# Small vectors on the ScalarE queue, the first key tile masked out of PSUM, and a table of priority offsets for the list scheduler

## Chip, cores and metric

The kernel runs on one core of a Trainium2 chip. The time is device microseconds of one execution; the median of three runs before the change is 300.35 us (300.14 to 301.22).

## What is computed

A token gate g mixes two branches over x (2048 tokens, 512 features). Branch A is attention with 32 heads of 16 in four segments of 512 tokens, plus a memory carried from segment to segment; branch B is a gated MLP with 1792 hidden features.

```python
g = sigmoid((x * gate_w).sum(-1, keepdims=True))
# branch A, per segment s; phi(t) = t + 1 if t > 0 else exp(t); gb = sigmoid(beta), one per head
p = softmax(qs @ ks.T * 0.25 + causal_mask);  a_dot = p @ vs
a_mem = (phi(qs) @ M) / (phi(qs) @ z + 1e-6)
o_s = gb * a_mem + (1 - gb) * a_dot
M += phi(ks).T @ vs;  z += phi(ks).sum()
a = concat(o_s) @ wo
# branch B
b = (gelu(x @ w_gate) * (x @ w_up)) @ w_down
return g * a + (1 - g) * b
```

## The kernel before

Everything works on one segment of 512 tokens at a time, features or heads on the 128 partitions. All work is written as tasks with reads and writes; a list scheduler, `Sched.schedule` (run while the kernel is built), picks for the earliest free engine the ready task with the highest priority, which is the longest chain of estimated times behind it plus the task's `bias`. The order that comes out is then fixed: each engine runs its own list in order and waits on semaphores where a task needs another engine. So whatever stands behind a waiting instruction on its engine waits too.

The tasks, by the functions in which they are written:

- `prep(s)`: projections K, Q (transposed, feature by token) and V, by `proj_T` and `pieces`, matmuls of line 408 into one of three rotating PSUM buffers `psW`, evicted by `copy_out` on ScalarE (line 422) or VectorE (line 425). K is then masked twice by `kp` (line 589 in the first segment, 597 later) into `kpad_0` and `kpad_1`, so that one 32-row matmul serves one head of two. The token gate (`gate`, `gexs`, `gts`), the transposed factors `exsT` (GpSimd) and `GdT`, and from the second segment on phi of Q (`pqe`, `pqc`), the denominator `den` (matmuls 128x8, then `ndsc` on VectorE) and four numerators `num` (matmuls 128x128, each evicted as `otok` on VectorE, line 657, and transposed by DMA into `oT`).
- `memory(s)`: phi of K, its DMA transposes `phkt`, the memory matmuls `mz` (128x136), added up and masked on VectorE (`mzacc`, `mzbd`).
- `attention(s)`: for each of four feature tiles t five passes A0, B0, C, A1, B1. A pass is score matmuls (`qk`, line 710) into the four banks `psXALL`, one exp of 128x2048 on ScalarE (line 718), and a causal mask on GpSimd (line 730). After B0 and C, and at the end, `pv` (line 743) multiplies with V into `psP`, VectorE transposes it (`tb`, line 751), and after both halves `norm` normalises: `recip`, `sc`, `obf`, `ott` and the add into `oT`, five VectorE instructions, lines 763 to 771.
- `gates_copied`, `gelu_phase`, `ups`, `downs`: the MLP, gate `G` (weights wg), gelu in one block per stage on ScalarE, up `U` (wu) with the product `Um` on VectorE (line 841), and down `D` together with the output projection (wd, wo), evicted as `ost` with the gate as scale (lines 866, 869).

The four stages are the four attentions; MLP and projections of the neighbouring segments fill TensorE between the passes.

At the start all loads stand in SP's list in the order of `rank`: x in two pieces, wk, wq, wv, then the small vectors `gatew`, `betab` (beta on every partition) and four `betaT` (beta in the order of the transposed heads), then the MLP weights (lines 438, 439) and the transposing loads of the second segment's x. `gexp` and `gexpT` (lines 546, 547) are exps of beta on ScalarE, counted among the first stage's exps so that one table load serves all; `gmat` is a chain of five VectorE operations behind them (lines 550 to 555).

Of the kernel before, what the change touches and what calls it, by code (L numbers as in the profile page):

```python
# [2 lines left out]

# [3 lines left out]
PE, ACT, DVE, POOL, SP = "pe", "act", "dve", "pool", "sp"  # L7
# [4 lines left out]
ACTF = mybir.ActivationFunctionType  # L12
# [7 lines left out]
P = 128  # L20
# [5 lines left out]
DMA_RATE = 330.0e3  # L26
PATIENCE = 3.0
OPEN_BONUS = 6.0
HOP = {PE: 0.17, ACT: 0.07, DVE: 0.07, POOL: 0.10, SP: 0.0}


# [38 lines left out]
class Task:  # L70


    def __init__(self, name, alts, grp=None, after=(), bias=0.0, nbytes=0):
        self.name = name
        self.alts = alts
        self.grp = grp
        self.after = tuple(after)
        self.bias = bias
        self.nbytes = nbytes
        self.tiled = None  # L80
        self.patience = 0.0
        self.ahead = False
        self.est = {e: sum(i.est for i in l) for e, l in alts.items()}
        rs, ws = set(), set()
        for l in alts.values():
            for i in l:
                rs.update(i.reads)
                ws.update(i.writes)
        self.reads, self.writes = rs, ws
        self.preds, self.succs = set(), set()  # L90
        self.prio = 0.0
        self.eng = None
        self.start = self.finish = None
        self.id = None
# [223 lines left out]
def act_t(n, psum=True, ap=False):  # L318
    return (0.167 if psum else 0.20) + n / 1200.0 + (0.093 if ap else 0.0)
# [15 lines left out]
def _build(es, nc, A_x, A_wq, A_wk, A_wv, A_wo, A_beta, B_w_gate, B_w_up, B_w_down, gate_w, out):  # L335
# [68 lines left out]
    def task(name, eng, instrs, **kw):  # L404
        return S.add(Task(name, {eng: instrs}, **kw))
# [12 lines left out]
    def copy_out(name, g, dst, src, reads, writes, n, engs=(ACT, DVE), **kw):  # L418

        alts = {}  # L420
        if ACT in engs:
            alts[ACT] = [Instr(lambda e: e.activation(dst(), src(), ACTF.Copy), reads=reads, writes=writes,
                               est=act_t(n))]
        if DVE in engs:
            alts[DVE] = [Instr(lambda e: e.tensor_copy(dst(), src()), reads=reads, writes=writes,  # L425
                               est=dve_t(n))]
        return S.add(Task(name, alts, grp=g, **kw))

    def dma(name, eng, out_ap, in_ap, reads, writes, nbytes, issue=0.7, transpose=False, bias=0.0, sm=None,
            nonc=False):  # L430
        sm = sm if sm is not None else sem("d")

        def f(e):
            if transpose:
                return e.dma_start_transpose(out_ap(), in_ap())
            if nonc:
                with nc.allow_non_contiguous_dma(reason="small vector"):
                    return e.dma_start(out_ap(), in_ap())  # L438
            return e.dma_start(out_ap(), in_ap())  # L439
        return task(name, eng, [Instr(f, reads, writes, issue, dma_sem=sm)], bias=bias, nbytes=nbytes)  # L440
# [3 lines left out]
    def wdma(key, eng, dst, src, nbytes, nonc=False):  # L444
        rank[0] -= 20.0
        dma("w_" + str(key), eng, lambda: dst, lambda: src, [], [("w", key)], nbytes, bias=rank[0], nonc=nonc)
# [28 lines left out]
    wdma("wk", SP, wk[:], r4(A_wk), 524288)  # L475
    wdma("wq", SP, wq[:], r4(A_wq), 524288)
    wdma("wv", SP, wv[:], r4(A_wv), 524288)
    wdma("gatew", SP, gatew[:], gate_w.rearrange("(kb p) -> p kb", p=P), 1024, nonc=True)
    wdma("beta", SP, betab[:], A_beta.partition_broadcast(P), 8192)
    for g in range(4):  # L480
        bsrc = A_beta.rearrange("(t g j) -> g t j", g=4, j=2)[g]
        rank[0] -= 20.0
        dma(f"betaT{g}", SP, lambda g=g: betaT[32 * g:32 * g + 32, :].rearrange("p (t j) -> p t j", j=2),
            lambda bsrc=bsrc: bsrc.partition_broadcast(32), [], [("betaT", g)], 1024, nonc=True, bias=rank[0])
    wdma(("wg", 0), SP, wg[:, :, 0:half], wgr[:, :, 0:half], 917504)
    wdma(("wg", 1), SP, wg[:, :, half:DF], wgr[:, :, half:DF], 917504)
    xdma(1)
# [67 lines left out]
        Instr(lambda e: e.tensor_tensor(gmat[:], gexp[:], gtmp[:], ALU.mult), [("c", "gexp"), ("c", "gtmp")],  # L555
              [("c", "gmat")], 0.2)])

    def proj_T(name, s, t, w, wkey, dst, wkeys):

        g = Grp(banks)  # L560
        xs = xT[s % NX]
        pieces(name, g, [mm(g, lambda: g.f32()[:, :], w[:, kb, t * 128:(t + 1) * 128], xs[:, kb, :],
                            [("xT", s % NX, kb), ("w", wkey)], kb == 0, kb == 3, 512) for kb in range(4)], 2)
        copy_out(name + "ev", g, lambda: dst[:, t, :], lambda: g.f32()[:, :], [g.key], wkeys, 512)

    def phi_task(nm, s, phase, src, skey, dst, dkey, i):
# [15 lines left out]
    def prep(s):  # L582
        sl, x3 = s % 2, s % NX
        ph = max(s - 1, 0)
        for t in range(4):
            proj_T(f"K{s}_{t}", s, t, wk, "wk", kT, [("kT", t)])
            if s == 0:
                task(f"kp{s}_{t}", DVE, [
                    Instr(lambda e, t=t, j=j: e.tensor_scalar(kpad[j][sl][:, t, :], kT[:, t, :], maskc[j][:, 0:1],
                                                              None, ALU.mult),  # L590
                          [("kT", t), ("c", "mask", j)], [("kpad", j, sl, t)], dve_t(512, 4, ap=True))
                    for j in range(2)])
            proj_T(f"Q{s}_{t}", s, t, wq, "wq", qT[sl], [("qT", sl, t)])
        if s > 0:
            for j in range(2):
# [385 lines left out]
```

## Time and profile before

| | |
|---|---|
| median of three runs | 300.35 us (300.14 to 301.22) |
| profiled execution, its own time | 301.33 us |
| its span, first to last instruction | 299.6 us |
| mean granted TensorE clock | 0.977 |
| busy: TensorE, ScalarE, VectorE, GpSimd | 277.6, 216.9, 192.0, 103.7 us |

A row of the trace names the line of the kernel, the engine and the tiles (output, arrow, inputs). A time in square brackets is how long the engine stood idle before, and what ended that. TensorE's clock is given as a share of 2.4 GHz; 0.50 is 1.2 GHz.

### The profile page before, as it was taken

The page shows a single profiled execution, that of the slowest core. Times are in us where ns is not written, and L with a number is a line of the kernel's source. Part 1 is how long each engine was busy: PE and PEld are TensorE (multiplying, and loading weights), DVE is VectorE, ACT ScalarE, POOL GpSimd, SP SyncE. Part 2 cuts the span into 40 slices and gives each one's busy share as a digit, 9 for nine tenths or more (in the row PEclk, how much of TensorE's full clock was granted, in tenths as well). Part 3 has the DMA queues.
Part 4 walks back from the last instruction along what each step waited for, and adds up shares of the span by engine and source line. Part 5 has one row for each costly group of instructions (what it writes and reads, how often), then busy time and mean ns, then how long its engine had stood idle before and what let it go on. Part 6 is the DMA issues. An engine that isn't in the chain of part 4 may idle for free.

```text
span 299.6 us, 5379 instructions
## 1 busy us (share of the span) xinstructions
PE 277.6 (93%) x2189; PEld 114.6 (38%) x2189; DVE 192.0 (64%) x333; ACT 216.9 (72%) x171; POOL 103.7 (35%) x193
## 2 busy tenths in 40 slices
PE   7459999999979999997899999999899999999995
PEld 3113433333434333443344433434344333343342
DVE  1036889868898864699643956479844636478440
ACT  3156988868999878796768897887878666686502
POOL 7002675434101333663200333385400334334300
PEclk9958999999999999999799999999999999999999
DMA  6299970000013421000300200100001200000002
GB/s 223 58 267 320 307 127 0 2 0 3 0 23 49 93 49 53 20 1 2 70 2 0 53 20 0 55 19 2 0 2 31 43 1 35 20 20 0 2 0 70
DMA packets 29737, 15.30 MB, mean 51 GB/s; under 512 B 21264, under 2 KB 29712, under 8 KB 29712
## 3 DMA queue, kind: packets, MB, share of 16 engines
q1 hardware_dynamic: 29712, 14.96, 20.2%
q8 instruction: 17, 0.28, 0.4%
q14 instruction: 8, 0.07, 0.1%
HBM read 8.14 MB, written 2.10 MB: 34 GB/s over the span
## 4 chain that ended last, share of the span: by engine, by line
PE 77%; DVE 7%; ACT 5%; DMA 3%; POOL 3%; SPq 2%; issue 2%; ACTq 0%; POOLq 0%
PE psW L408 62%; PE psXALL L710 8%; PE psP L743 6%; ACT pt L718 4%; DMA betaT<-in_A_beta_dram 3%; POOL pt L730 1%; SPq L439 1%; PE psXALL L408 1%; DVE otok L657 1%; POOL exsT L625 1%; DVE kpad_1 L597 1%; SPq L438 1%; DVE ndsc L646 1%; DVE hT L841 1%; DVE tb L751 0%
## 5 line engine op out<-in xcount | busy, mean ns | idle before, releaser
L718 ACT ACTIVATE pt<-psXALL 128x2048 bf16<-128x2048 f32 x80 | 150.1, 1877 | 46.2 <-PE psXALL L710 34.5
L730 POOL TENSOR_SCALAR_AFFINE_SELECT pt<-pt 128x512 bf16<-128x512 bf16 (+1 forms) x112 | 83.8, 750 | 176.1 <-ACT pt L718 167.8
L408 PE MATMUL psW<-xT,wu 128*128 128x512 bf16 x224 | 52.8, 380 | 1.0 <-DVE mzacc L683 0.7
L408 PE MATMUL psW<-xT,wg 128*128 128x512 bf16 x224 | 51.6, 381 | 0.0
L408 PE MATMUL psW<-wd,hT 128*128 128x512 bf16 x210 | 51.6, 380 | 0.0
L841 DVE TENSOR_TENSOR hT<-psW,hT 128x512 bf16<-128x512 f32 x56 | 37.5, 686 | 14.3 <-PE psW L408 14.0
L751 DVE STREAM_TRANSPOSE tb<-psP 128x512 f32<-128x512 f32 x32 | 22.8, 713 | 34.9 <-PE psP L743 34.8
L408 PEld LDWEIGHTS psW<-xT,wg 128*128 128x128 bf16 x224 | 20.6, 98 | 26.1 <-issue 2.0
L408 PEld LDWEIGHTS psW<-xT,wu 128*128 128x128 bf16 x224 | 20.1, 98 | 25.8 <-issue 2.7
L408 PEld LDWEIGHTS psW<-wd,hT 128*128 128x128 bf16 x210 | 18.6, 98 | 23.4 <-issue 4.3
L743 PE MATMUL psP<-pt,vaug 128*17 128x256 bf16 (+3 forms) x512 | 23.8, 306 | 0.6 <-POOL pt L730 0.6
L710 PE MATMUL psXALL<-qT,kpad_0 32*128 32x512 bf16 (+3 forms) x256 | 16.3, 308 | 8.1 <-DVE gtmp L553 7.3
L820 ACT ACTIVATE hT<-psW 128x512 bf16<-128x512 f32 x28 | 16.3, 597 | 6.8 <-PE psW L408 6.8
L710 PE MATMUL psXALL<-qT,kpad_1 32*128 32x512 bf16 (+3 forms) x256 | 16.1, 305 | 2.5 <-ACT pt L718 2.5
L408 PE MATMUL psW<-wv,xT 128*128 128x512 bf16 x64 | 17.8, 421 | 0.4 <-DVE vaug L425 0.4
L408 PE MATMUL psW<-xT,wq 128*128 128x512 bf16 x64 | 16.0, 381 | 0.5 <-DMA wq<-in_A_wq_dram 0.5
L425 DVE CAST hT<-psW 128x512 bf16<-128x512 f32 x22 | 14.5, 677 | 2.6 <-PE psW L408 2.5
L408 PE MATMUL psW<-wo,oT 128*128 128x512 bf16 x60 | 15.9, 380 | 0.0
L408 PE MATMUL psW<-xT,wk 128*128 128x512 bf16 x64 | 15.5, 380 | 0.2 <-DMA wk<-in_A_wk_dram 0.2
L743 PEld LDWEIGHTS psP<-pt,vaug 128*17 128x17 bf16 x512 | 10.1, 90 | 14.1 <-issue 6.8
L625 POOL COPY exsT<-exs 32x4 f32<-32x4 f32 x64 | 14.2, 222 | 3.7
L710 PEld LDWEIGHTS psXALL<-qT,kpad_0 32*128 32x128 bf16 x256 | 4.5, 92 | 25.3 <-ACT pt L718 13.2
(92 smaller groups left out, 249.9 us busy)
## 6 DMA issues: line engine op xcount, KB each, us to landing
out_dram<-ost SPq DMA_DIRECT2D x16, 128.0 KB, 1.7
wg<-in_B_w_gate_dram SPq DMA_DIRECT2D x2, 896.0 KB, 13.4
wu<-in_B_w_up_dram SPq DMA_DIRECT2D x2, 896.0 KB, 6.4
wd<-in_B_w_down_dram SPq DMA_DIRECT2D x1, 1792.0 KB, 12.7
hT<-in_A_x_dram SPq DMA_DIRECT2D x2, 256.0 KB, 2.8
wk<-in_A_wk_dram SPq DMA_DIRECT2D x1, 512.0 KB, 5.2
wq<-in_A_wq_dram SPq DMA_DIRECT2D x1, 512.0 KB, 6.2
wv<-in_A_wv_dram SPq DMA_DIRECT2D x1, 512.0 KB, 7.1
```

The source lines that it names most:

```text
L408: return Instr(lambda e: e.matmul(view(), lhsT, rhs, start=first, stop=last), reads=reads, writes=[fkey if fkey is not None else g.key], e ...
L425: alts[DVE] = [Instr(lambda e: e.tensor_copy(dst(), src()), reads=reads, writes=writes, est=dve_t(n))]
L438: return e.dma_start(out_ap(), in_ap())
L439: return e.dma_start(out_ap(), in_ap())
L625: cross = task(f"exsT{s}", POOL, [Instr(lambda e, g=g, c=c: e.tensor_copy(exsT[sl][32 * g:32 * g + 32, c:16:4], exs[32 * c:32 * c + 32, s4 ...
L710: instrs.append(Instr(lambda e, t=t, g=g, j=j, kb=kb, ncol=ncol, c0=c0: e.matmul(X[g][:, c0:c0 + ncol], kpad[j][sl][32 * g:32 * g + 32, t, ...
L718: prev_exp[0] = exp_task(s, f"exp{s}_{t}{name}", [Instr(lambda e: e.activation(PT[slot][:], XALL[:, :].rearrange("p (g c) -> p g c", g=4), ...
L730: minstrs.append(Instr(lambda e, view=view, pat=pat: e.affine_select(out=view, in_=view, compare_op=ALU.is_ge, fill=0.0, base=0, pattern=p ...
L743: instrs.append(Instr(lambda e, q=q, kb=kb, slot=slot, c0=c0, h=h: e.matmul(Pb[32 * q:32 * q + 17, 128 * kb:512], Vaug[sl][:, kb, h, :], P ...
L751: task(f"pvt{s}_{t}_{j}", DVE, [Instr(lambda e: e.transpose(Tb[i2][:, j, :], Pb[:, :]), [("P",)], [("Tb", i2, j)], dve_t(512))])
L820: lambda e, g=g, ft=ft, s=s: e.activation(hT[s % 2][:, ft, :], g.f32()[:, :], ACTF.Gelu_apprx_tanh),
L841: task(f"Um{s}_{ft}", DVE, [Instr(lambda e, g=g, ft=ft: e.tensor_tensor(hT[sl][:, ft, :], g.f32()[:, :], hT[sl][:, ft, :], ALU.mult), [g.k ...
```

## The change

Three things change.

First, the six small loads are issued by ScalarE's queue in place of SP's, and in another order: `betab`, four `betaT`, then `gatew`. ScalarE issues them before its first table load.

Second, the first K tile of the first segment is evicted twice by ScalarE: once through `kpad_0`'s mask as a scale column, straight from PSUM into `kpad_0`, and once as before into `kT`. The VectorE task that made both masks makes only `kpad_1` for that tile.

Third, a table `BIAS` of 89 numbers, keyed by the name of a task up to the first underscore or dot (kind and segment), is added to the priorities. The instructions and their sizes stay as they were.

```diff
+BIAS = {
+    "D1": 28, "D2": -81, "D3": -30, "G1": -23, "G2": -26, "G3": 129, "GdT0": 14, "GdT1": 24, "GdT3": -43,
...
-        self.bias = bias
+        self.bias = bias + BIAS.get(name[:re.search(r"[_.]|$", name).start()], 0.0)
...
-    wdma("gatew", SP, gatew[:], gate_w.rearrange("(kb p) -> p kb", p=P), 1024, nonc=True)
-    wdma("beta", SP, betab[:], A_beta.partition_broadcast(P), 8192)
+    wdma("beta", ACT, betab[:], A_beta.partition_broadcast(P), 8192)
     for g in range(4):
...
-        dma(f"betaT{g}", SP, lambda g=g: betaT[32 * g:32 * g + 32, :].rearrange("p (t j) -> p t j", j=2),
-            lambda bsrc=bsrc: bsrc.partition_broadcast(32), [], [("betaT", g)], 1024, nonc=True, bias=rank[0])
+        dma(f"betaT{g}", ACT, lambda g=g: betaT[32 * g:32 * g + 32, :].rearrange("p (t j) -> p t j", j=2),
+            lambda bsrc=bsrc: bsrc.partition_broadcast(32), [], [("betaT", g)], 1024, nonc=True, bias=rank[0],
+            issue=0.5)
+    wdma("gatew", ACT, gatew[:], gate_w.rearrange("(kb p) -> p kb", p=P), 1024, nonc=True)
...
-    def proj_T(name, s, t, w, wkey, dst, wkeys):
+    def proj_T(name, s, t, w, wkey, dst, wkeys, even=None):
...
+        if even is not None:
+            task(name + "even", ACT, [Instr(lambda e: e.activation(even[0], g.f32()[:, :], ACTF.Copy,
+                                                                   scale=maskc[0][:, 0:1]),
+                                            [g.key, ("c", "mask", 0)], [even[1]], act_t(512, ap=True))], grp=g)
...
-            proj_T(f"K{s}_{t}", s, t, wk, "wk", kT, [("kT", t)])
+            first = s == 0 and t == 0
+            proj_T(f"K{s}_{t}", s, t, wk, "wk", kT, [("kT", t)],
+                   even=(kpad[0][sl][:, t, :], ("kpad", 0, sl, t)) if first else None)
...
-                    for j in range(2)])
+                    for j in ((1,) if first else (0, 1))])
```

Where the order moves, in three places. First, ScalarE at the start of the program, before:

```order
L467 ACT_TABLE_LOAD
L467 ACTIVATE stmp<-pt 128x1
L422 ACTIVATE xT<-psW 128x512 x2
L422 ACTIVATE kT<-psW 128x512
L546 ACTIVATE gexp<-betab 128x32
L547 ACTIVATE gexpT<-betaT 128x8
L422 ACTIVATE qT<-psW 128x512
L422 ACTIVATE kT<-psW 128x512
L718 ACTIVATE pt<-psXALL 128x2048
```

and with the change:

```order
L452 DMA betab<-in_A_beta_dram 128x32
L451 DMA betaT<-in_A_beta_dram 32x4x2 x4
L451 DMA gatew<-in_gate_w_dram 128x4x1
L480 ACT_TABLE_LOAD
L480 ACTIVATE stmp<-pt 128x1
L435 ACTIVATE xT<-psW 128x512 x2
L560 ACTIVATE gexp<-betab 128x32
L561 ACTIVATE gexpT<-betaT 128x8
L579 ACTIVATE kpad_0<-psW,maskc 128x512
L435 ACTIVATE kT<-psW 128x512 x2
L738 ACTIVATE pt<-psXALL 128x2048
```

Six DMA issues stand ahead of the table load, and the exps of beta stand ahead of every eviction of K. On VectorE the five `gmat` operations now stand ahead of the cast of the first Q tile, which VectorE has in place of ScalarE; on TensorE the first score matmuls come after 12 projection matmuls and 2 of V, before after 16 projection matmuls.

Second, TensorE between the last `pv` of the first stage and the second stage's passes (psW<-xT,wu is an up projection, psW<-vaug,phkt is `mz`, psW<-mzbd,phq 128x8 is `den` and 128x128 is `num`, wd and wo are the down part), before:

```order
L408 MATMUL psW<-vaug,phkt 128x136 x16
L408 MATMUL psW<-xT,wu 128x512 x12
L408 MATMUL psW<-mzbd,phq 128x8 x16
L408 MATMUL psW<-xT,wu 128x512 x4
L408 MATMUL psW<-mzbd,phq 128x128 x16
L408 MATMUL psW<-xT,wu 128x512 x28
L710 MATMUL psXALL<-qT,kpad_1 128x384 x4
```

and with the change:

```order
L421 MATMUL psW<-xT,wu 128x512 x52
L421 MATMUL psW<-vaug,phkt 128x136 x16
L421 MATMUL psW<-gatew,xT 128x1 x16
L421 MATMUL psW<-wo,oT 128x512 x4
L421 MATMUL psW<-wd,hT 128x512 x2
L421 MATMUL psW<-wo,oT 128x512 x2
L730 MATMUL psXALL<-qT,kpad_1 128x384 x4
L730 MATMUL psXALL<-qT,kpad_1 128x128 x4
L421 MATMUL psW<-wo,oT 128x512 x2
L421 MATMUL psW<-wd,hT 128x512 x2
L421 MATMUL psW<-mzbd,phq 128x8 x16
L421 MATMUL psW<-wd,hT 128x512 x4
```

All up projections come first (the four missing matmuls stand just above), `mz` after them, and `den` and the four `num` go between down projections, after the next passes of scores. K and V of the second segment, which stood just ahead of these rows, were moved forward into the first stage.

Third, TensorE at the end of the second stage, from `den` on, before:

```order
L408 MATMUL psW<-mzbd,phq 128x8 x16
L408 MATMUL psW<-xT,wu 128x512 x6
L710 MATMUL psXALL<-qT,kpad_1 128x256 x8
L408 MATMUL psW<-mzbd,phq 128x128 x4
L408 MATMUL psW<-xT,wu 128x512 x2
L710 MATMUL psXALL<-qT,kpad_1 128x512 x4
L408 MATMUL psW<-mzbd,phq 128x128 x12
L710 MATMUL psXALL<-qT,kpad_1 128x384 x4
```

and with the change, from the last `pv` row after `den` on:

```order
L763 MATMUL psP<-pt,vaug 17x128 x4
L421 MATMUL psW<-mzbd,phq 128x128 x12
L730 MATMUL psXALL<-qT,kpad_1 128x256 x8
L421 MATMUL psW<-mzbd,phq 128x128 x4
L730 MATMUL psXALL<-qT,kpad_1 128x512 x4
L421 MATMUL psW<-xT,wu 128x512 x6
L730 MATMUL psXALL<-qT,kpad_1 128x384 x4
```

Three `num` groups come at once and take all three buffers; the next up projection stands behind the fourth. VectorE's list has one `otok`, the five instructions of `norm`, then three `otok`, in both. In the third stage K, V and Q of the last segment and 9 of the 14 up groups of the third come ahead of its end, 12 up matmuls standing between its last C and A1 scores where 6 stood; `mz`, `den` and `num` of the last segment go into the fourth stage; and at that stage's end 10 matmuls of the down part stand between the last C and A1 scores where 4 up matmuls stood.

## Rows read from the trace of the kernel before

**Rows 1.** Page, busy time of the whole span: us, share, instructions of each engine.

```profile
PE 277.6 (93%) x2189; PEld 114.6 (38%) x2189; DVE 192.0 (64%) x333; ACT 216.9 (72%) x171; POOL 103.7 (35%) x193
```

**Rows 2.** Table by stretch: busy us per engine (instructions), PEclk, DMA share, GB/s.

```profile
11.40:14.00 2.60, 0.00 (x0) 0.00 (x0) 0.00 (x0) 0.14 (x1) 0.00 (x0) 1.00 0.04 0
14.00:18.65 4.65, 0.00 (x0) 0.03 (x1) 0.53 (x4) 0.83 (x3) 0.00 (x0) 0.52 0.69 260
18.65:24.40 5.75, 5.75 (x23) 1.72 (x24) 3.79 (x10) 3.25 (x4) 0.65 (x1) 0.50 1.36 209
80.00:90.00 10.00, 7.50 (x58) 3.46 (x56) 9.74 (x20) 10.00 (x5) 0.00 (x0) 1.00 0.10 20
140.00:144.00 4.00, 0.83 (x9) 0.33 (x8) 3.93 (x6) 3.19 (x2) 1.20 (x2) 0.98 0.00 0
144.00:147.30 3.30, 3.29 (x34) 1.40 (x35) 2.75 (x5) 1.34 (x1) 0.54 (x1) 0.50 0.41 83
200.00:214.00 14.00, 12.38 (x133) 5.42 (x135) 12.54 (x22) 10.74 (x8) 8.08 (x14) 1.00 0.01 1
...
274.00:280.00 6.00, 4.85 (x32) 1.83 (x31) 5.46 (x10) 4.43 (x3) 2.86 (x3) 1.00 0.00 0
```

**Rows 3.** Chain of waits, start of the program: start, us, what.

```profile
7.22 10.48 DMA betaT<-in_A_beta_dram
```

**Rows 4.** Timeline, 0 to 24 us: start, us, engine, line, instruction, idle before.

```profile
0.81 1.28 ACT L467 ACT_TABLE_LOAD   x1 [0.81 <-PEq L966]
...
3.42 0.68 SPq L438 DMA_DIRECT2D gatew<-in_gate_w_dram  x1
...
4.14 1.60 SPq L439 DMA_DIRECT2D betab<-in_A_beta_dram  x1
...
5.78 1.87 SPq L438 DMA_DIRECT2D betaT<-in_A_beta_dram  x4
...
8.59 1.04 PE L408 MATMUL psW<-xT,wq 128*128 128x512 bf16 x4 [0.48 <-DMA wq<-in_A_wq_dram]
...
11.31 0.23 ACT L546 ACTIVATE gexp<-betab 128x32 f32<-128x32 bf16 x1 [2.56 <-DMA betab<-in_A_beta_dram]
17.82 0.21 ACT L547 ACTIVATE gexpT<-betaT 128x8 f32<-128x8 bf16 x1 [6.28 <-DMA betaT<-in_A_beta_dram]
...
18.06 0.17 DVE L550 TENSOR_SCALAR gexpT<-gexpT 128x8 f32<-128x8 f32 x1 [8.66 <-ACT gexpT L547]
...
18.65 0.62 PE L710 MATMUL psXALL<-qT,kpad_0 32*128 32x512 bf16 x4 [7.30 <-DVE gtmp L553]
18.93 0.19 DVE L555 TENSOR_TENSOR gmat<-gexp,gtmp 128x32 f32<-128x32 f32 x1
...
19.57 0.68 DVE L425 CAST qT<-psW 128x512 bf16<-128x512 f32 x1
...
22.45 1.14 SPq L439 DMA_DIRECT2D wu<-in_B_w_up_dram  x2
```

**Rows 5.** Page, DMA issues: tiles, queue, count, KB each, median us to landing.

```profile
out_dram<-ost SPq DMA_DIRECT2D x16, 128.0 KB, 1.7
...
wu<-in_B_w_up_dram SPq DMA_DIRECT2D x2, 896.0 KB, 6.4
...
hT<-in_A_x_dram SPq DMA_DIRECT2D x2, 256.0 KB, 2.8
```

**Rows 6.** Timeline of TensorE, after the first stage.

```profile
88.47 6.22 PE L408 MATMUL psW<-xT,wu 128*128 128x512 bf16 x28 [0.19 <-DVE otok L657]
```

**Rows 7.** Timeline of VectorE, end of the second stage.

```profile
137.15 0.72 DVE L751 STREAM_TRANSPOSE tb<-psP 128x512 f32<-128x512 f32 x1 [0.31 <-PE psP L743]
...
139.28 0.34 DVE L763 RECIPROCAL recip<-tb 128x32 f32<-128x32 f32 x1
...
141.47 1.29 DVE L771 TENSOR_TENSOR oT<-oT,ott 128x512 bf16<-128x512 bf16 x1
...
142.68 0.68 DVE L657 TENSOR_TENSOR otok<-psW,ndsc 128x512 bf16<-128x512 f32 x1
```

More of the change, by code (lines that the diff above doesn't have):

```diff
@@ L1 @@
+import re
 from contextlib import ExitStack
@@ L28 @@
 OPEN_BONUS = 6.0
+BIAS = {
[10 rows of a table added]
+}
 HOP = {PE: 0.17, ACT: 0.07, DVE: 0.07, POOL: 0.10, SP: 0.0}
```

9 rows, old and new, of the table BIAS are left out of this document.

## The prediction

> **What bounds the kernel now.** Read first, on the page, the shares of busy time: TensorE is busy 93% of the span [rows 1]. So two things are worth having: stretches in which it stands idle, and stretches in which its clock is low. The table by stretch shows where they are [rows 2]: TensorE does nothing from 11.40 to 14.00; from 14.00 to 18.65 the clock falls to its lower level (1.2 of 2.4 GHz); from 18.65 to 24.40 TensorE is fully busy, but at 0.50. Later 2.5 us of 80:90 are idle, 3.2 of 140:144 (with the clock at 0.50 until 147.30), 1.6 of 200:214, 1.15 of 274:280. Everywhere else TensorE is full, so what is taken out of these stretches reaches the end.
>
> The chain of waits explains the first: the last betaT transfer takes 10.48 us from its issue at 7.22 to landing [rows 3]. gexpT on ScalarE waits for it until 17.82, VectorE's gate chain follows, and the first scores start at 18.65, after 7.30 us without a matmul [rows 4]. In 11.40:14.00 the DMA engines are 4% busy: the transfer is not short of bandwidth. It stood behind x and three weights on the same queue (betab, just ahead of it, was used at 11.31) and then takes some 6.4 us itself, being made of tiny pieces.
>
> **Part 1: six small vectors go to ScalarE's queue.** On SP they take from 3.42 to 7.65 to issue, 4.2 us [rows 4]. On ScalarE they are issued from 0.81 (where its table load now starts) to about 5.0, betaT's last at about 3.9. The table load (1.28) ends at 6.3 instead of 2.1, so ScalarE's two evictions of x end near 7.7 instead of 6.2. That is covered: the second projection cannot start before wq lands, at 8.59. SP issues the gate weights 4.2 us earlier; nobody waits for them now, so no gain is counted.
>
> When does betaT land? Call it T. Not before 3.9 plus 1.7, the shortest landing in the trace [rows 5], so 5.6; not after 3.9 plus the 10.48 of today, 14.4. I take the sequence seen: betab, issued first, lands like the first x load 2.8 us after 0.81, at 3.6, and betaT follows in the 6.4 us that separate the two now (11.31 to 17.70). T = 10.0.
>
> Who waits for it? ScalarE's order puts gexp and gexpT ahead of the evictions of the first K tile, and VectorE's now has the five gate operations ahead of the cast of the first Q tile. So the first scores come at T plus 0.12 (hand-over), 0.24 (gexpT), 1.06 (18.06 to the end of gmat at 19.12), 0.68 (the cast) and a hand-over of 0.1: T + 2.2 [rows 4]. At T = 10 that is 12.2, 6.45 us earlier than 18.65. Two projection matmuls fewer are done by then (14, not 16, at 0.22 each, as the 28 in 6.22 us [rows 6]): minus 0.45. **6.0 us.**
>
> **The clock.** TensorE's work before the wait ends near 10.5 (Q at 9.65, four matmuls of K behind it), and V's first matmuls run at T + 1.6 = 11.6. Now it had stood still from 11.4 for 2.8 us before the clock fell; a gap of one us should not do it. The 5.75 us at 0.50 [rows 2] would be 2.9 at full clock, but VectorE has 3.8 us of work in the same stretch, so it shrinks to 3.8 at best. **2.0 us** (ends 0 and 2.9).
>
> **Part 2: the first K tile masked out of PSUM.** One ScalarE eviction with a scale column, like ost's, replaces one of VectorE's two small masks. Both stand inside T + 2.2 (ScalarE is through by T + 1.6, VectorE later). Nothing; without the wait for betaT it would save the hop over kT, at most 0.5 us.
>
> **Part 3: BIAS changes the order.** The work is the same; what counts is what stands in front of each wait.
> - After the first attention stage (80:90, 2.5 us idle) den and num stood among the first up projections, and each waited for VectorE's chain of mzacc, mzbd and ndsc. Now all 14 up groups run first, and num comes one by one between down projections. ScalarE, full for all of 80:90, still gates the next scores within 0.3 us. **2.2 us.**
> - End of the second stage (140:144, 3.2 us idle). The normalisation that holds VectorE from 139.28 to 142.76 [rows 7] still stands between the first num eviction and the other three, and the up groups that filled the time ahead of it are gone. From the PV matmul to the next free PSUM buffer there are a transpose, two evictions (0.7 each), the normalisation (3.5) and hand-overs, 5.8 us, against some 1.7 of TensorE work (the num matmuls and two passes of scores): 4.1 idle at worst, 3.2 if it costs no more than now. I take 3.7: **minus 0.5 us**, and the clock falls there again.
> - End of the third stage (200:214, 1.6 us idle). K, V and Q of the last segment are done earlier, den and num move into the last stage, and 12 up matmuls (2.7 us) stand where 6 stood, against an exp of 1.88. Nothing is left there to wait. **1.6 us.**
> - End of the last stage (1.15 us idle). Between the two scores that waited there are now 10 down matmuls (2.25 us) for 4 of up. **1.1 us.** The last output tile ends as before.
>
> **Sum.** 6.0 + 2.0 + 2.2 - 0.5 + 1.6 + 1.1 = 12.4 us, of which the order has 4.4. The profiled execution took 301.33 (span 299.6), so 288.9; it stood 0.98 above the median of 300.35, so the median is forecast at **287.9 us**. With T between 8.5 and 11.5 and 1 us either way in the order, this case spans 285.5 to 290.5.
>
> **Rivals.**
> *Early landing, 284.5 us.* With T under 8.2 the start is bound by Q: its matmuls end at 9.65, the cast ends at 10.3, scores at 10.4. That is 18.65 - 10.4 - 0.45 + 2.0 = 9.8; and if the denser order keeps the clock up at 144.00:147.30, half of 3.3 us comes back: 9.8 + 4.4 + 1.65 = 15.85. For it: the pieces are small and start ahead of most of the bulk. Against: the 6.4 us that they take with idle engines. Chance 0.20.
>
> *Only the issue moves, 294.3 us.* T = 14.4, first scores at 16.55: 18.65 - 16.55 - 0.45 = 1.65; the clock falls as now and gives nothing; with the order's 4.4, 6.05 us. The 4% in 11.40:14.00 speaks against it; that x and the weights move on SP's queue in the same time speaks for it. Chance 0.10. The Trainium skill ("DMA: Bandwidth & Descriptors", section "Issuing engines are not separate DMA queues") speaks for this one: DMAs started by different engines run on the same 16 engines and interleave, and several issuers save only the issue time. By that, the total would be this 294.3 instead of 287.9.
>
> *The table of numbers brings nothing, 292.4 us.* It was fitted to the planner's costs; where the chip's differ, new stalls can eat the 4.4 us and only the start's 8.0 remain. Against: the stalls removed are rows of the trace. Chance 0.10.
>
> *Slower, 305.2 us.* The one mechanism: the betaT wait now stands in front of the evictions that free TensorE's buffers, and the bulk behind it starts 4.2 us earlier. If the bulk queue starves the small pieces until the up weights land (issued until 23.59, second at about 23.0, plus 6.4, less 4.2 [rows 4, 5]), T is 25.2 and scores start at 27.4: 18.65 - 27.4 - 0.45 = -9.2, plus 4.4. The sign turns at T = 20.4, and the loss passes half a per cent (1.5 us, about what a measurement of this kernel can tell from no change) at 21.9. For it: with both on one queue, the small pieces of now landed only when the bulk ahead of them had. Against: this bulk stands on another queue. Chance 0.03, and 0.03 for a T just short of it.
>
> **How the numbers follow.** The forecast has 0.54. The range, 283.5 to 293.5, takes in the early landing and the useless table, and leaves out the issue-only rival, the slow ones and strays, 0.2 at most. Faster 0.94, same 0.03, slower 0.03.
>
> **What would show it.** gexpT starting at about 10 and first scores two us later; granted clock 1.00 from there to 24; no idle TensorE between the first stage's end and the next scores; three to four us idle, and a low clock behind, at the end of the second stage; none over half a us later. Wrong would be: gexpT after 14, a first score matmul that waits for something else than the gate chain, or new waits on VectorE's otok and hT of together more than 5 us.

## The result and the profile after

The changed kernel takes **293.03 us** (median of 4 runs, 292.16 to 293.62), the kernel before beside it 300.79 (4 runs, 300.14 to 302.94): a ratio of 0.973, 95% interval 0.967 to 0.979. The forecast was 287.9 in 283.5 to 293.5. Faster was right, and the time is just inside the range, 5 us from the forecast. The profiled execution took 292.53 (span 290.8), that of before 301.33 (299.6): 8.8 us, where the sum of steps had 12.4. So 3.6 of the 5 us are steps that came out smaller; the rest is that the profiled execution lay 0.98 above its median before and 0.5 below it after.

Page of the kernel after, busy time, as [rows 1] of before: TensorE is as full as it was.

```profile
PE 272.3 (94%) x2150; PEld 114.2 (39%) x2189; DVE 191.3 (66%) x332; ACT 217.5 (75%) x172; POOL 103.0 (35%) x193
```

Its table by stretch (columns as in [rows 2]): the start, then the end of the first, second, third and last stage. The page counts 2189 weight loads and 2150 matmuls: 39 matmuls have no record, so a part of what looks idle in this trace is not.

```profile
10.00:12.20 2.20, 0.16 (x2) 0.02 (x2) 0.34 (x3) 0.62 (x2) 0.00 (x0) 1.00 0.99 261
12.20:13.50 1.30, 1.30 (x4) 0.47 (x5) 0.63 (x4) 0.77 (x2) 0.00 (x0) 0.51 0.71 258
13.50:14.50 1.00, 1.00 (x4) 0.39 (x3) 0.39 (x1) 0.00 (x0) 0.00 (x0) 0.50 1.08 372
...
16.10:24.00 7.90, 7.85 (x51) 3.23 (x52) 6.78 (x13) 7.11 (x6) 1.92 (x3) 1.00 1.25 224
69.00:86.50 17.50, 17.29 (x111) 7.57 (x106) 14.08 (x24) 17.39 (x10) 1.27 (x2) 1.00 0.00 0
86.50:100.00 13.50, 12.22 (x129) 5.99 (x132) 11.53 (x22) 10.41 (x10) 7.07 (x21) 1.00 0.42 69
...
133.00:139.60 6.60, 2.46 (x37) 1.28 (x30) 6.46 (x11) 5.32 (x3) 2.38 (x3) 0.92 0.10 20
139.60:142.00 2.40, 2.39 (x9) 0.72 (x12) 1.43 (x3) 0.02 (x1) 0.64 (x1) 0.52 0.40 82
...
196.00:210.00 14.00, 13.79 (x118) 5.46 (x112) 13.59 (x22) 11.75 (x8) 7.61 (x11) 1.00 0.00 1
...
268.00:276.00 8.00, 7.55 (x63) 3.13 (x64) 4.11 (x7) 5.71 (x4) 3.50 (x4) 1.00 0.05 17
```

The wait for betaT that stood in the chain [rows 3] is gone, and another load has its place:

```profile
2.33 9.81 DMA wq<-in_A_wq_dram
12.14 0.05 issue
12.19 4.01 PE psW L421 x10
16.20 0.33 PE psXALL L730 x4
```

The timeline of the start, as [rows 4], shows why:

```profile
0.81 0.42 ACTq L452 DMA_DIRECT2D betab<-in_A_beta_dram  x1
...
1.26 2.10 ACTq L451 DMA_DIRECT2D betaT<-in_A_beta_dram  x4
...
3.38 2.04 ACTq L451 DMA_DIRECT2D gatew<-in_gate_w_dram  x1
...
5.46 1.28 ACT L480 ACT_TABLE_LOAD   x1 [5.46 <-issue]
...
11.58 0.21 ACT L561 ACTIVATE gexpT<-betaT 128x8 f32<-128x8 bf16 x1 [2.86 <-DMA betaT<-in_A_beta_dram]
...
12.19 1.89 PE L421 MATMUL psW<-xT,wq 128*128 128x512 bf16 x4 [2.04 <-DMA wq<-in_A_wq_dram]
...
16.13 0.40 PE L730 MATMUL psXALL<-qT,kpad_0 32*128 32x512 bf16 x4
```

betaT is there 6 us earlier (gexpT at 11.58, before at 17.82), but wq, which TensorE used at 8.59 before, comes at 12.14. TensorE stands idle for 2.04 us ahead of it, and what follows runs at the lower clock: the ten projection matmuls up to the first scores take 4.01 us. The page's DMA issues, as [rows 5], have every large load of the start later; before, x took 2.8, wk 5.2, wv 7.1 and wq:

```profile
wq<-in_A_wq_dram SPq DMA_DIRECT2D x1, 512.0 KB, 6.2
```

Now:

```profile
hT<-in_A_x_dram SPq DMA_DIRECT2D x2, 256.0 KB, 5.0
wk<-in_A_wk_dram SPq DMA_DIRECT2D x1, 512.0 KB, 7.2
wq<-in_A_wq_dram SPq DMA_DIRECT2D x1, 512.0 KB, 9.8
wv<-in_A_wv_dram SPq DMA_DIRECT2D x1, 512.0 KB, 12.5
```

**A ruler.** The program has 80 exps of scores on ScalarE, 20 per stage, in the same order in every kernel here. The lead of a run is how much earlier an exp starts than in the kernel before; the tail is the time from the start of the last exp to the end. The gain in the span is the lead of the last exp plus what the tail has lost. Leads and tails are taken from the start times in the profiled executions; wq is the landing on the page, from the issue. Each row is one execution: for "queue alone" it lay 0.9 us above that run's median, for "no betaT + norm late" 1.3 above it (the slowest of six).

| run | wq | lead: 1st exp | 4th | end of stage 1 | end of stage 2 | last | tail |
|---|---|---|---|---|---|---|---|
| before | 6.2 | 0 | 0 | 0 | 0 | 0 | 18.2 |
| after | 9.8 | 2.71 | 4.76 | 5.39 | 3.49 | 4.47 | 13.8 |
| queue alone | 11.2 | 0.89 | 3.36 | 3.12 | 1.60 | 1.08 | 18.2 |
| order alone | 7.8 | -0.61 | -0.01 | 0.63 | -1.44 | -1.27 | 13.8 |
| no betaT | 7.5 | 6.64 | 8.69 | 9.10 | 7.03 | 8.01 | 13.8 |
| no betaT, gatew back | 6.5 | 7.36 | 9.41 | 10.06 | 7.98 | 8.27 | 13.8 |
| pieces doubled | 10.6 | 0.19 | 2.24 | 2.72 | 0.65 | 1.21 | 13.8 |
| old mask | 11.2 | 1.28 | 3.33 | 3.98 | 2.09 | 3.08 | 13.8 |
| norm late | 11.1 | 0.74 | 2.64 | 3.28 | 3.63 | 4.61 | 13.8 |
| gate late, on before | 6.7 | 7.04 | 9.51 | 4.13 | 3.93 | 2.82 | 18.1 |
| no betaT + norm late | 6.7 | 7.36 | 9.41 | 10.06 | 9.49 | 9.46 | 13.8 |
| the same + gate late | 7.6 | 6.63 | 8.68 | 8.42 | 9.80 | 10.78 | 13.8 |
| the same + keys late | 7.1 | 7.14 | 9.19 | 8.92 | 9.56 | 10.07 | 13.8 |

So in this execution the start gave the changed kernel 4.8 us (forecast 8.0) and the order 8.8 - 4.8 = 4.0 (forecast 4.4). The order's part is a tail shorter by 4.3, less 0.3 of lead. My reading is that TensorE's filler work, which no longer waits in the stages, isn't left over behind the last exp.

### The profile page after: what moved, and what is told of

Same layout as the page of the kernel before. It is cut to its first block, busy times and chain, and to the rows that moved or that the text cites. A ratio compares the mean times of both kernels' runs of the same rounds, so it can differ in the third digit from the quotient of the medians.

```text
span 290.8 us, 5337 instructions
## 1 busy us (share of the span) xinstructions
PE 272.3 (94%) x2150; PEld 114.2 (39%) x2189; DVE 191.3 (66%) x332; ACT 217.5 (75%) x172; POOL 103.0 (35%) x193
## 4 chain that ended last, share of the span: by engine, by line
PE 79%; DVE 9%; ACT 5%; DMA 3%; issue 2%; POOL 1%; SPq 0%; ACTq 0%
PE psW L421 64%; PE psXALL L730 8%; PE psP L763 6%; ACT pt L738 5%; DMA wq<-in_A_wq_dram 3%; PE psXALL L421 1%; DVE tb L771 1%; DVE kpad_1 L617 1%; DVE hT L861 1%; DVE otok L677 1%; POOL pt L750 1%; DVE kT L597 1%; DVE ost L889 0%; SPq L452 0%; DVE pex L595 0%
## 5 line engine op out<-in xcount | busy, mean ns | idle before, releaser
L421 PE MATMUL psW<-xT,wu 128*128 128x512 bf16 x216 | 52.1, 386 | 2.8 <-DVE otok L677 2.1
L421 PE MATMUL psW<-xT,wg 128*128 128x512 bf16 x217 | 50.7, 380 | 0.8 <-ACT hT L840 0.2
L421 PE MATMUL psW<-wd,hT 128*128 128x512 bf16 x203 | 50.5, 380 | 0.5 <-issue 0.2
L730 PE MATMUL psXALL<-qT,kpad_1 32*128 32x512 bf16 (+3 forms) x256 | 15.8, 301 | 2.6 <-ACT pt L738 2.6
L421 PE MATMUL psW<-xT,wk 128*128 128x512 bf16 x61 | 16.2, 396 | 0.3 <-DVE sc_1 L785 0.2
L421 PE MATMUL psW<-wv,xT 128*128 128x512 bf16 x61 | 15.7, 381 | 0.3 <-DVE vaug L438 0.2
L438 DVE CAST hT<-psW 128x512 bf16<-128x512 f32 x20 | 13.5, 683 | 3.8 <-PE psW L421 3.4
L730 PE MATMUL psXALL<-qT,kpad_0 32*128 32x512 bf16 (+3 forms) x256 | 15.8, 301 | 0.1
L421 PE MATMUL psW<-wo,oT 128*128 128x512 bf16 x54 | 14.6, 380 | 0.6 <-issue 0.3
L829 ACT ACTIVATE hT<-hT 128x2048 bf16<-128x2048 bf16 (+2 forms) x6 | 12.7, 2185 | 0.0
## 6 DMA issues: line engine op xcount, KB each, us to landing
wg<-in_B_w_gate_dram SPq DMA_DIRECT2D x2, 896.0 KB, 13.1
```

Of the source, the lines that this page charges most:

```text
L421: return Instr(lambda e: e.matmul(view(), lhsT, rhs, start=first, stop=last), reads=reads, writes=[fkey if fkey is not None else g.key], e ...
L730: instrs.append(Instr(lambda e, t=t, g=g, j=j, kb=kb, ncol=ncol, c0=c0: e.matmul(X[g][:, c0:c0 + ncol], kpad[j][sl][32 * g:32 * g + 32, t, ...
L829: t = task(f"gelu{s}_{f0}", ACT, [Instr(lambda e, hv=hv: e.activation(hv, hv, ACTF.Gelu_apprx_tanh), hk, hk, act_t(512 * n, False) + (0.0 ...
```

## The experiments

Theory A: the loads of 2 to 4 bytes a piece hold up the large ones wherever they fly together, so the start lost on wq part of what it won on betaT. Rival B: a second queue as such does it. Rival C: ScalarE, busy with issuing, is late with its evictions. The edits are shown in short; `...` stands for what is left out.

**1. The queue alone.** The kernel before with its order; only the six small loads moved.

```diff
-    wdma("gatew", SP, ...); wdma("beta", SP, ...); dma(f"betaT{g}", SP, ...)
+    # first on ACT: beta, betaT0 to betaT3, gatew; every other instruction in the order of before
```

> The kernel before with its order of work kept, only the six small loads (betab, four betaT, gatew) issued by ScalarE ahead of its other work instead of by SyncE behind wv. The page of the changed kernel puts 4.8 us of the gain at the start (the gap of the exp instructions at the end of the first block) and 4.0 us at the later places. If the two parts are independent, this kernel takes about 296 us and its exps keep a lead of 4 to 5.5 us over the kernel before from the first block to the end. My forecast had 8 us for the start; it would give 292.5. If the start's gain needs the new order (first block's order is another in the changed kernel), it is under 2 us: over 298.5.

Measured: 299.36 us, ratio 0.991 (0.988 to 0.995), 2.6 us. Less than the 4.8, and the 296 expected was missed: in this execution wq landed after 11.2 us, 1.4 later than in the run after, and the lead of the 4th exp is smaller by those 1.4. betaT came later, too:

```profile
13.62 0.21 ACT L547 ACTIVATE gexpT<-betaT 128x8 f32<-128x8 bf16 x1 [2.00 <-DMA betaT<-in_A_beta_dram]
```

Then the old order's wait after the first stage (1.3 us idle in 80:84 and 0.5 in 84:86) ended at the lower clock, where it had stayed up in the kernel before ([rows 2], 80:90 at 1.00), and 1.6 us of the lead went:

```profile
84.00:86.00 2.00, 1.47 (x10) 0.74 (x11) 2.00 (x5) 2.00 (x2) 0.00 (x0) 0.81 0.32 65
86.00:88.00 2.00, 1.78 (x5) 0.72 (x5) 1.18 (x2) 1.98 (x2) 0.00 (x0) 0.50 0.35 71
```

**2. The order alone.** The changed kernel, its six small loads back on SyncE behind wv, its order else kept.

```diff
-    # on ACT, first: beta, betaT0 to betaT3, gatew
+    # on SP behind wv: gatew, beta, betaT0 to betaT3
```

> The changed kernel with its order of work kept, only the six small loads put back on SyncE behind wv. If order and start are independent: betaT lands near 17.7 us and the first scores run near 18.7 as before, and what is left is the order's gain of about 4.0 us: 296.8 us. If the order's gain comes only with the early start, 299 to 301. Sizes of the stages: lead of the exps over the kernel before about 0 in the first block, near -0.5 us at its end, 4 us at the last.

Measured: 297.97 us (296.8 expected), ratio 0.989 (0.982 to 0.995), 3.4 us. The lead is never above 0.6 us and ends at -1.3; the whole gain is the tail, 18.2 to 13.8. The two parts alone make 2.6 + 3.4 = 6.0 of the 8.2 that the ratio of both makes; the other 2.2 fit what each alone lost to waits and the lower clock on the way (1.6 us of lead after the first stage above; here 1.6 from the last exp but one of the second stage to the first of the third, where after lost 0.65), but that was not tried by itself.

**3 and 4. Fewer tiny pieces.** gexpT needs nothing that gexp doesn't have: four small VectorE operations pick it out, and the four betaT loads go. In the second run gatew is back on SyncE behind wv, too.

```diff
-    for g in range(4): dma(f"betaT{g}", ACT, ...)          # and the exp of betaT
-    tensor_scalar(gexpT, gexpT, 1.0, add)
+    for g in range(4): tensor_scalar(gexpT[32*g:32*g+32], gexp[32*g:32*g+32, g-th pairs], 1.0, add)
-    wdma("gatew", ACT, ...)                                # second run only
+    wdma("gatew", SP, ...)                                 # behind wv
```

> The changed kernel without the four betaT loads; gexpT is picked out of gexp by four small VectorE copies instead. betab and gatew stay on ScalarE's queue. Theory A (pieces of 2 to 4 bytes, wherever they are issued, take the DMA engines from the large loads): wq landed at 9.81 us with betaT, 4-byte and 2-byte pieces in flight; without betaT's it lands between 7 and 8.5 us, the first scores run near 12 to 13, and the kernel takes about 289.5 us (3.5 less). Rival B (any second queue, or SyncE's slower issues, delays the large loads): wq still lands after 9.3, the first scores run after 15, 292 to 293.5. Rival C (ScalarE's late start, behind its issues, sets the start and no landing does): wq may land early but the first scores stay after 15.

> As the run without betaT, and gatew back on SyncE behind wv, so that only betab's one load is on ScalarE's queue. Theory A: nothing but betab's 128 short pieces is beside the large loads, wq lands near 6.5 us after a start like that of the kernel before (its landing of x 2.8 us after the issue), the first scores run at 10.5 to 12, the clock does not fall before them, and the time is 286 to 288 us. Under A gatew's 2-byte pieces are a part of the delay, so this run is faster than the one without betaT by 0.5 to 2 us; if betaT's are all of it the two are equal. Rival B: wq after 9 us, 292 to 293.5.

Measured: 289.61 us (ratio 0.960, 0.955 to 0.964) and 288.21 (0.955, 0.951 to 0.960). Theory A's numbers hold, but that the time of the second run is 0.2 us above its range: wq lands after 7.5 and 6.5 us (in the lines below, first without betaT, then with gatew back as well), TensorE's clock stays at 1.00 through the start, and the first scores run at 12.21 and 11.49.

```profile
wq<-in_A_wq_dram SPq DMA_DIRECT2D x1, 512.0 KB, 7.5
wq<-in_A_wq_dram SPq DMA_DIRECT2D x1, 512.0 KB, 6.5
```

Without betaT, from the start of the second projection:

```profile
9.94 1.04 PE L421 MATMUL psW<-xT,wq 128*128 128x512 bf16 x4
...
12.21 0.39 PE L724 MATMUL psXALL<-qT,kpad 32*128 32x512 bf16 x4
```

Against 12.19 and 16.13 of the run after, wq is 2.25 us earlier and the ten matmuls in between take 2.3 us instead of 4.0: the lower clock cost 1.7. What the pieces do to the large loads can be seen in the DMA view of 4.00 to 5.00 us, of after and then of the run with gatew back (total, then the queue of SyncE and that of ScalarE: packets, MB, share of 16 engines):

```profile
DMA packets 148, 0.06 MB, mean 64 GB/s; under 512 B 86, under 2 KB 148, under 8 KB 148
...
q1 hardware_dynamic: 70, 0.06, 18.3%
q10 hardware_dynamic: 78, 0.00, 3.5%
```

```profile
DMA packets 387, 0.37 MB, mean 368 GB/s; under 512 B 28, under 2 KB 387, under 8 KB 387
...
q1 hardware_dynamic: 381, 0.37, 108.0%
q10 hardware_dynamic: 6, 0.00, 0.3%
```

With pieces in flight 70 packets of SyncE's queue get through where 381 do without them, while the engines are 22% busy. It is not one large packet for each small one: in the same us of the run without betaT, 56 of SyncE's went beside 276 of ScalarE's, where gatew's pieces were on the way. Rival B falls for wq: the second queue is still there with betab on it. x does pay for betab: 4.5 us from the issue in the run with gatew back, 2.8 before. No run put large pieces on the second queue: whether any traffic there that lasts as long would do the same is left open.

**5. Twice the pieces.** Four more loads like betaT's, their data read late in the first stage. They are written between betaT and gatew, but were issued behind gatew, at 5.36, so the dose came later than meant.

```diff
+    for g in range(4): dma(f"betaU{g}", ACT, ...)          # issued behind gatew; gts1 depends on it
```

> The changed kernel with four more loads like betaT's on ScalarE's queue, between betaT and gatew; their data are read only at the end of the first block. Theory A (the short pieces take the DMA engines from the large loads): wq's landing, 9.81 us after its issue in the changed kernel and 7.52 without betaT, moves by about as much again, to 11.5 to 13, the first scores run at 18 to 20 instead of 16.1, and the time is 295 to 297 us, 2 to 3.5 slower than the changed kernel. Rival B (the second queue as such): wq lands at 9.8 as before, the time stays within 1 us of 293.

Measured: 295.86 us, ratio 0.982 (0.977 to 0.987), 2.8 slower than after, as expected, but not in the way expected: wq landed at 10.6, inside what the same loads show without the extra ones (9.8 to 11.2). ScalarE was late instead:

```profile
1.25 2.48 ACTq L452 DMA_DIRECT2D betaT<-in_A_beta_dram  x4
3.77 1.57 ACTq L452 DMA_DIRECT2D gatew<-in_gate_w_dram  x1
5.36 5.48 ACTq L452 DMA_DIRECT2D betaU<-in_A_beta_dram  x4
10.88 1.28 ACT L481 ACT_TABLE_LOAD   x1 [10.88 <-issue]
...
12.28 1.06 ACT L436 ACTIVATE xT<-psW 128x512 bf16<-128x512 bf16 x2
```

An issue takes longer while many pieces are still on their way (5.48 us for the four of betaU, 2.48 for betaT's; gatew's took 0.46 in the run without betaT); what holds it isn't shown. The evictions of x stand behind it, and TensorE stood idle for 5.4 us until 12.91 for the first of them. So rival C is a second mechanism, and it decided this run, with its still larger number of pieces; the extra ones came too late for wq and fell on the gate weights (15.4 us from issue instead of 13.1). The dose says nothing clean on A; runs 3 and 4 do.

**6. The old mask.** The second part of the change undone: the first key tile's mask from kT on VectorE again, same order.

```diff
-    activation(kpad[0][0][:, 0], K0_0 in PSUM, Copy, scale=maskc[0])       # ScalarE, ahead of kT
+    tensor_scalar(kpad[0][0][:, 0], kT[:, 0], maskc[0], mult)              # VectorE, behind the cast of qT
```

> The changed kernel with the one masked copy of the first key tile made on VectorE from kT again, as before, in the same order otherwise; ScalarE evicts kT straight away, 0.67 us earlier. I forecast this part at nothing, since the first scores wait for qT and a slow TensorE then: the first scores within 0.5 us of 16.1 and the time within 0.7 us of the changed kernel. If the part was worth something, the first scores run 0.7 to 1.3 us later (VectorE's qT cast, then 0.3 us of mask in front of them) and the time is 1 us longer.

Measured: 294.75 us, ratio 0.977 (0.973 to 0.982); after had 0.973 (0.967 to 0.979). The time is 1.7 us above the changed kernel's, where at most 0.7 was expected, and the first scores are 1.4 later, where at most 0.5 was. The profiled one is 1.4 us slower, and wq says why: it landed 11.24 us after its issue. From there on nothing differs; the matmuls up to the scores take the 4.01 us of the run after:

```profile
2.33 11.24 DMA wq<-in_A_wq_dram
13.57 0.05 issue
13.62 4.01 PE psW L421 x10
17.63 0.33 PE psXALL L730 x4
```

So between wq and the scores the mask part is worth nothing, as forecast; whether the other three executions had a late wq as well isn't shown.

**7. The normalisation late.** At the end of the second stage VectorE normalises in front of the last three otok evictions, which free TensorE's buffers. Here they change places, in the changed kernel.

```diff
     nump2_0
-    norm1_2
     nump2_1, nump2_2, nump2_3
+    norm1_2
```

> The changed kernel with one task moved on VectorE: at the end of the second block the normalisation of the attention output (five operations, 3.3 us) runs behind the three otok evictions that free PSUM banks, not in front of them. My reading of the wait of 2.05 us for otok at 139.6: TensorE loses about 3 us there and runs some 2 us at the lower clock afterwards. If that is right the wait for otok goes, the exps behind it gain 2 to 2.5 us, and with the clock the kernel takes 289.5 to 291.5 us. Rival: the exps set that place, and the wait for pt grows by what the wait for otok loses: within 0.5 us of 293.

Measured: 292.25 us, ratio 0.971 (0.965 to 0.977), above the 289.5 to 291.5 expected: by time alone not to be told from after. By place it is: this execution had wq 1.3 us later (11.1) and was 2.1 behind after until this point, and no longer behind it. From the last exp but one of the stage to its last, after loses 0.7 of its lead and this run wins 1.5; its clock doesn't fall there (it does for 3.4 us in the run after). TensorE's waits, of after and of this run:

```profile
137.16 0.39 PE L730 MATMUL psXALL<-qT,kpad_1 32*128 32x512 bf16 x4 [1.51 <-ACT pt L738]
139.61 2.34 PE L421 MATMUL psW<-xT,wu 128*128 128x512 bf16 x5 [2.05 <-DVE otok L677]
```

```profile
139.22 0.39 PE L730 MATMUL psXALL<-qT,kpad 32*128 32x512 bf16 x4 [1.51 <-ACT pt L738]
139.55 1.47 PE L421 MATMUL psW<-xT,wu 128*128 128x512 bf16 x6
141.74 0.40 PE L730 MATMUL psXALL<-qT,kpad 32*128 32x384 bf16 x8 [0.72 <-ACT pt L738]
```

Together with no betaT and gatew back:

> The best of the start (no betaT, gatew behind wv: 288.2 us) with the normalisation behind the otok evictions at the end of the second block. If the two are independent and the second is worth 2 to 3.5 us: 284.7 to 286.2 us. If the wait for otok is only exchanged for another: 288.

Measured: 286.27 us (6 runs), ratio 0.949 (0.946 to 0.953), 1.9 less than without it and just above the range expected; its six times all lie below the other's four. That is where the gain shows in time.

**8. The gate's readers late.** Who needs betaT at the first scores? Nobody: its readers, and only by their place in two in-order queues. In the kernel *before*, all loads left on SyncE:

```diff
     # ScalarE: gexp, gexpT from ahead of the second eviction to ahead of the first exs (gexs0)
     # VectorE: the five gate operations from ahead of the key masks to ahead of the first gdT (GdT0)
```

> The kernel before, all loads on SyncE as they were, with only two small tasks later in their engines' order: the two exponentials of the gate on ScalarE in front of the first exs instead of in front of the second eviction, and the five small gate operations on VectorE in front of the first gdT, their first reader, instead of in front of the key masks. Theory: the first scores do not need betaT; they waited for it because its readers stood ahead of their evictions in two in-order queues. Then with betaT still landing near 17.7 us the first scores run at 10.8 to 11.8, the exps lead the kernel before by 8.5 to 9.5 us in the first block, and the time is 291 to 293.5 us; 1.6 us less of the lead if the clock falls after the first block as it did in the run of the queue alone. Rival: something else of the start needs betaT, and the first scores stay after 16: over 297 us.

Measured: 298.28 us, ratio 0.988 (0.983 to 0.993), not the 291 to 293.5 expected. The first half of the theory holds: first scores at 11.81, a lead of 9.5 us at the 4th exp. By the end of the stage 5.4 of it is lost, on x of the next segment, whose transfer stands behind the tiny pieces on SyncE's queue; the clock falls with it (0.54 in 24 to 30 us):

```profile
11.81 0.40 PE L710 MATMUL psXALL<-qT,kpad 32*128 32x512 bf16 x4
...
22.39 1.08 PE L408 MATMUL psW<-xT,wq 128*128 128x512 bf16 x2 [1.48 <-DMA xT<-in_A_x_dram]
24.91 1.89 PE L408 MATMUL psW<-xT,wq 128*128 128x512 bf16 x4 [1.44 <-DMA xT<-in_A_x_dram]
```

In the kernel before, no wait for x of that segment stands among TensorE's: the one for betaT will have covered it. In both places the pieces cost their time, on wq from ScalarE's queue and on the next x from SyncE's: in these two kernels the place chose which load pays.

**9. No load on ScalarE's queue.** The run of 286.27 with betab behind gatew on SyncE and the gate's readers late; then the same with three operations on the keys moved behind the second otok eviction at the start of the second stage.

```diff
-    w_beta on ACT, gexp and gmat first
+    w_beta on SP behind w_gatew; gexp ahead of gexs0, gmat ahead of GdT0
-    nump1_0, pkc1_0, nump1_1                               # second run only
+    nump1_0, nump1_1, pkc1_0
```

> The best kernel so far (no betaT, normalisation behind the otok evictions, 286.27 us) with betab on SyncE behind gatew, so that no load is on ScalarE's queue, and the gate's exponential and small operations late as in the run on the kernel before. Theory A: even betab's 128 pieces held up x (4.5 us to land instead of 2.8), and the gate operations stood in front of the evictions of x; without both the first projection starts when wk lands, near 7 us, the first scores run at 10 to 10.6 instead of 11.55, and the time is 284.5 to 285.8 us. Rival B: the start of the engines sets x's landing, the first scores stay at 11.5 and the time at 286.3.

> As the run before it, and at the start of the second block the three key feature operations on VectorE (3.0 us) behind the second otok eviction, not in front of it. The wait of 1.12 us for otok there should go: 0.8 to 1.2 us faster than the run before it, 283.5 to 285. If the wait only moves to the next otok, whose eviction then comes 0.6 us later, the gain is under 0.4.

Measured: 286.03 us (ratio 0.948, 0.942 to 0.954) and 286.85 (0.951, 0.947 to 0.955, 6 runs). Neither is told from 286.27. In the first, x landed after 3.1 us, not 4.6, but wk after 6.6 instead of 5.7 and wq after 7.6 instead of 6.7, so the first scores ran at 12.22, not at 10. What A said of x came, the time it forecast didn't. In the second the wait moved, as its rival said: it is nearly as long as before, at the next eviction, and the run it is compared with had only 0.4 us of it left.

```profile
96.21 0.41 PE L421 MATMUL psW<-mzbd,phq 128*128 128x128 bf16 x4 [1.01 <-DVE otok L671]
```

The fastest kernels of the study are thus those without betaT's loads and with the normalisation late, 286.0 to 286.3 us, 5% under the kernel before and 2.3% under the changed one.

## Why the prediction was right, and where it was not

- **Direction: right, and the order's part with it.** The wait for betaT was the largest idle stretch, it left the chain, and the order came nearly as summed. The start did not: 4.8 for 8.0. That the time fell inside the range is partly luck: the upper end was drawn to take in a useless table, not slower loads, and the time is 0.5 us below it.
- **The sign "a first score matmul that waits for something else than the gate chain" came true:** wq, at 12.14, stands ahead of it.
- **T = 10.0:** gexpT ran at 11.58, so T was 11.5, 1.5 later and between the bounds of 5.6 and 14.4. This was the earliest of four executions with the same loads; in runs 6 and 7 gexpT ran at 13.43 and 13.35, in run 1 at 13.62. betaT's last load was issued at 2.7, not 3.9, and landed 8.8 us later; in the other three 10.6 to 10.8, against 10.48 before. So betaT gained mostly the 4.5 us of its earlier issue. The 6.4 us that I put behind betab's landing were too few: they measured 7.1, and 9.3 in run 1.
- **The step that failed** is "That is covered: the second projection cannot start before wq lands, at 8.59". It took the landings of the large loads as fixed and asked only who waits for the small ones. They fly together: wq came at 12.14. With T = 11.5 the chain T + 2.2 would have had the first scores at 13.7; they ran at 16.13. The chain itself holds where wq is there in time: in run 2 gexpT starts at 16.81 and the scores at 19.24, 2.4 later for the 2.1 summed, since the mask on VectorE stands behind the cast. Without betaT's loads the scores run at 12.21, close to the forecast by chance: nothing waits for betaT there. Of the 3.9 us in between, 2.25 are wq's landing and 1.7 the clock.
- **"A gap of one us should not do it"** fell with it: the gap was 2.04 us, and the clock was at 0.51 from 12.20 on. The term itself, 2.0 us, came to its size although the clock did fall: the lead grows from 2.71 to 4.76 from the first exp to the fourth, because the clock is back at 1.00 by 16.10, where it stayed at 0.50 to 24.40 before [rows 2]. So the start's first term measured 2.7, not 6.0.
- **The mask out of PSUM:** nothing on the path from wq to the scores, as forecast (run 6).
- **The order,** 4.4 forecast, 4.0 measured. After the first stage 2.2 were forecast; a new wait of 1.15 us for otok left some 1.2. End of the second stage: -0.5 forecast, -0.7 in the lead from the last exp but one to the last (4.21 to 3.49), with 4.1 us idle where 3.7 were forecast; the normalisation in front of three evictions was named as the cause [rows 7], and run 7 shows it. End of the third: 1.6 idle before, 0.2 now. End of the last: 1.15 before, at most 0.45 now. These make some 2.6 to 3.0, and up to 0.45 comes from a shorter stretch at the lower clock (2.4 us, before 3.3); the rest, 0.6 to 0.9, I can't place, since records are missing.
- **The rivals.** The useless table, 292.4 us, is nearest in time and not what happened: the order brought 4.0, and 3.4 by itself (run 2); what is missing is missing at the start. "Only the issue moves", 294.3, was nearly right on how long betaT takes from issue to landing; its T of 14.4 came from too late an issue, and it had no word on wq. The Trainium skill ("DMA: Bandwidth & Descriptors", section "Issuing engines are not separate DMA queues"), on which it leant, says that DMAs of several issuers interleave on the same 16 engines and that only issue time is saved. The first half agrees with the trace, 70 packets of one queue beside 78 of the other in one us, and it is the half that I should have priced. The second half agrees nearly: the issue came 4.5 us earlier and gexpT 6.2 us in the run after, 4.2 in run 1. By the same page (section "Queues, rings and completion order") an engine serves the queues that have work in turn, packet by packet; the 70 and 78 would fit that, the 56 and 276 of the run without betaT fit it less well, and no run here decides it. The slower rival had the mechanism the wrong way round: the bulk didn't starve the pieces, the pieces slowed the bulk.

## What to carry to other kernels

Cost a load by its pieces, not its bytes: some 3 KB (betaT's four of 0.5 and gatew's 1.0) in 2- and 4-byte pieces, on a queue of their own, held up a load of 512 KB on the other by 3.3 us (wq after 9.8, without them 6.5), and on one queue the transfer behind them (run 8). First ask whether such a load is needed at all (here it was a permutation of one already on the chip), then who shares the DMA engines with it. Where a chain shows a long wait, ask whether the waiting instruction needs the data or only stands in front of one that doesn't; and before counting the gain, look for the transfer that is next behind it.

## What the hardware showed that was not expected

- Tiny pieces are slow with the engines nearly idle: 148 packets in a us at 22% busy, about half of them large, against 387 at 108% that are nearly all large; in the kernel before, alone, at 4% [rows 2].
- gatew's issue on ScalarE took 0.46 us behind betab alone and 2.04 behind betaT's pieces; ScalarE's table load came behind it, at 1.75 and 5.46.
- The same loads in the same order land differently from one execution to the next: wq after 9.8, 11.1, 11.2 and 11.2 us with the pieces in flight (the run after, runs 7, 1 and 6). Those 1.4 us are as much as the changed kernel's times spread (1.5); that they are the reason isn't shown. In the runs without betaT's pieces on the second queue it was 6.2 to 7.8.
- Nearly the same idle time after the first stage, 2.5 and 2.8 us of 76:90, left the clock at 1.00 in the kernel before and took it to 0.50 in run 1: a wait of this size may or may not bring the clock's price with it, so it is safer gone.
